# Splitting the first tile's window sums over VectorE and Pool, later softmax, one Exp, and new planner costs in a three-layer kernel

## The chip, the cores and the metric

The kernel runs on one core of one Trainium2 chip. The metric is the device time in microseconds of one execution; lower is better. Engines are named as in the profile: PE (TensorE, matrix products), DVE (VectorE), ACT (ScalarE), POOL (GpSimd, "Pool" in the text) and SP (SyncE, which issues all transfers here).

## What is computed

Three layers in a row on x of shape 2 x 4160 x 192, all float32:

```
w = softmax(weight_gen over its 7 taps)                 # [2, 4160, 8 heads, 7]
a[s] = sum over k of w[s, head, k] * x[s - 6 + k]       # a window of 7 rows, per head
prev = a shifted by one row
xk = mu_k * a + (1 - mu_k) * prev ;  xr = mu_r * a + (1 - mu_r) * prev
y = sigmoid(xr @ w_r) * (relu(xk @ w_k)**2 @ w_v)       # 192 -> 1024 -> 192
h = relu(y @ w_in) ;  c = 3-tap convolution of h along the rows, per channel
out = (h * sigmoid(c)) @ w_out                          # 192 -> 1024 -> 192
```

## The kernel before

**Tiles.** The 4160 rows are cut into ten tiles: 256, 248, seven of 472 and one of 352 rows, each for both batches. A tile holds 2, 2, 4, ..., 4, 3 "slots" per batch, one row of x per partition in each. For one slot and batch, `token` computes the window sum in four elementwise instructions: a product of 128 x 1344 elements (rows times softmax weights) into the scratch tile `prod`, and three sums of 576, 384 and 192 elements, the last into `tok`. `attention` loads the rows of one tile and batch in one transfer and issues its tokens; all of them run on Pool.

**From tokens to matrix products.** `mixing(i, u, ...)` transposes `tok` on PE for one of three column groups (u = 0: batch 0; u = 2: what is left of both batches; u = 1: batch 1), mixes each row with the one before it, and splits the results into a high and a low part (`hi` on ACT, `lo` on DVE or Pool), so that a float32 product can be made of several fp32r products. For u = 2 the parts are also moved between partitions by transfers into `xB`. `moe1` is one of eight 128-channel chunks of the second layer (PE into `pa`, ACT and DVE into `s`, PE into `am` and `ar`), `moe2` the same for the third layer (`pc`, `h`, `g`, `bm`, `br`).

**Weights.** The weights arrive as 64-bit numbers in `stage` and are converted on the chip: for each of 16 pieces, `narrow` is one ACT copy and five DVE instructions, and `split` adds an ACT copy and a DVE subtraction per part. `wkA`, `wkB`, `wv`, `wrA`, `wrB` serve `moe1`, `wiA`, `wiB`, `wo` serve `moe2`.

**Softmax.** It is done in four parts: tile 0, tile 1, tile 2, and tiles 3 to 9. Each part has the steps maximum (DVE reduce), subtract, Exp (ACT), sum (DVE reduce), a small add and a reciprocal (DVE), and multiply. Subtract and multiply run on DVE for tile 0 and on Pool otherwise. For tiles 3 to 9 the steps are issued in seven groups, one per tile, each with an Exp of its own; the scratch of these groups lies in `stage`, which the weight conversion uses first. ACT has Exp and Sigmoid in different tables, so an Exp between two chunks of `moe2` brings two table loads.

**Order.** Nothing is issued directly. Each step is put in a list with a due time (`at(t, fn, hold)`, where one unit is one chunk of `moe1`); negative times are the prologue. `Program.schedule` then plans the whole program with estimated costs: at each moment it takes the engine that can start first, and on it the ready instruction with the lowest due time. `hold` is an earliest planned time in microseconds. The plan decides only the order of instructions on each engine; on the chip every engine runs its list in order and waits for data. The plan treats Pool instructions and those DVE instructions that read two SBUF operands (or copy SBUF to SBUF) as excluding each other (`shares`, `port`).

The lines that set the prologue are these:

```
softmax(0, 0, slots[0], DVE, (-95, -94.9, ...), am_r.tiles[0])
attention(0, 0, -99.9, -90, 0.1, POOL)
attention(0, 1, -99.6, -83.7, 0.1, POOL)
prepare((-99.75, -99.7, -99.4), [(-82, chunk_rem(w_k, wkB, True)), (-81, chunk_in(w_k, wkA, 0)), (-0.5, chunk_out(w_v, wv, 0)), ...
```

Of the kernel before, what the change touches and what calls it, by code (L numbers as in the profile page):

```python
# [24 lines left out]
WIN = KS * DM  # L25
NF = DFF // 128
LAG = 10


def f(ap):  # L30
# [3 lines left out]
class Program:  # L34
# [37 lines left out]
    def cost(self, eng, method, out, ins, pointer):  # L72

        n = self.count(out)
        src = [self.space(x) for x in ins]
        if method == "dma_start":
            return 0.6, 0.0
        if eng == "PE":
            busy = max(n * 0.00045 + 0.002, 0.109)
            return busy, busy + 0.24  # L80
        if eng == "ACT":
            near = bool(src) and src[0] == "PSUM"
            p = 0.1 if pointer else 0.0
            return (0.06 if near else 0.09) + p + n / 1200, (0.2 if near else 0.24) + p + n / 1200
        if eng == "DVE":
            if method == "tensor_reduce":
                n = self.count(ins[0])
            if method == "reciprocal":
                return 0.07 + n / 160, 0.2 + n / 160
            if method in ("tensor_scalar", "tensor_copy", "memset") and "PSUM" not in src:  # L90
                return 0.07 + n / 1920, 0.2 + n / 1920
            stt = method == "scalar_tensor_tensor"
            return (0.13 if stt else 0.07) + n / 960, (0.26 if stt else 0.2) + n / 960
        if eng == "POOL":
            busy = 0.1 + (n / 455 if method == "tensor_tensor" else n / 270)
            return busy, busy + 0.12
        return 0.6, 0.6

    def schedule(self):
        n = len(self.ops)  # L100
        succ, left, ready, dur, late, moved = [[] for _ in range(n)], [0] * n, [0.0] * n, [0.0] * n, [0.0] * n, [0.0] * n
        shares = [False] * n
        log = {}
        for i, (eng, method, a, k, _, hold) in enumerate(self.ops):
            ready[i] = hold
            aps = [x for x in [*a, *k.values()] if hasattr(x, "tensor") and hasattr(x, "ap")]
            out = k["out"] if "out" in k else aps[0]
            ins = [x for x in aps if x is not out]
            dur[i], late[i] = self.cost(eng, method, out, ins, any(x is not None and x in ("scale",) and hasattr(k[x], "tensor") for x in k))
            if method == "dma_start":  # L110
                moved[i] = self.count(out) * out.ap[0][1] * 4 / 240e3 if self.space(out) != "DRAM" else self.count(ins[0]) * ins[0].ap[0][1] * 4 / 240e3

            src = [self.space(x) for x in ins if self.count(x) > 1]
            shares[i] = eng == "POOL" or eng == "DVE" and (
                src == ["SBUF", "SBUF"] or method in ("tensor_scalar", "tensor_copy") and self.space(out) == "SBUF" and src == ["SBUF"])
            before = set()
            for x, write in [(x, False) for x in ins] + [(out, True)]:
                name, p0, p1, f0, f1 = self.region(x)
                seen = log.setdefault(name, [])
                keep = []  # L120
                for e in seen:
                    j, w, q0, q1, g0, g1 = e
                    if (w or write) and p0 < q1 and q0 < p1 and f0 < g1 and g0 < f1:
                        before.add(j)
                        if write and p0 <= q0 and q1 <= p1 and f0 <= g0 and g1 <= f1 and j != i:
                            continue
                    keep.append(e)
                keep.append((i, write, p0, p1, f0, f1))
                log[name] = keep
            before.discard(i)  # L130
            left[i] = len(before)
            for j in before:
                succ[j].append(i)
        free = dict.fromkeys(self.real, 0.0)
        port, table = 0.0, None
        wires = dict.fromkeys(self.real, 0.0)
        open_ = {e: [] for e in self.real}
        for i in range(n):
            if not left[i]:
                open_[self.ops[i][0]].append(i)  # L140
        start = [0.0] * n
        for _ in range(n):
            t, eng = min((max(free[e], min(ready[i] for i in w)), e) for e, w in open_.items() if w)
            i = min((i for i in open_[eng] if ready[i] <= t), key=lambda i: (self.ops[i][4], i))
            open_[eng].remove(i)
            if shares[i]:
                t = max(t, port)
                port = t + dur[i]
            turn = 0.0
            if eng == "ACT" and self.ops[i][1] == "activation" and self.ops[i][2][2] in (ACTF.Exp, ACTF.Sigmoid):  # L150
                turn = 0.0 if self.ops[i][2][2] == table else 1.3
                table = self.ops[i][2][2]
            start[i] = t
            free[eng] = t = t + turn
            free[eng] += dur[i]
            end = t + late[i]
            if self.ops[i][1] == "dma_start":
                wires[eng] = max(wires[eng], t + dur[i] + 0.6) + moved[i]
                end = wires[eng] + 0.8
            for j in succ[i]:  # L160
                ready[j] = max(ready[j], t + dur[i] if eng == "PE" == self.ops[j][0] else end)
                left[j] -= 1
                if not left[j]:
                    open_[self.ops[j][0]].append(j)
        for i in sorted(range(n), key=lambda i: (start[i], i)):
            eng, method, a, k = self.ops[i][:4]
            getattr(self.real[eng], method)(*a, **k)  # L167
# [14 lines left out]
def conv_moe_kernel(ctx: ExitStack, tc: tile.TileContext, xp, wg_first, wg_rest, mus, w_k, w_v, w_r, w_in, conv_w, w_out, out):  # L182
# [11 lines left out]
    def ring(name, n, shape, dtype=F32):  # L194
        return Ring([new(f"{name}{j}", shape, dtype) for j in range(n)])
# [28 lines left out]
    rows_r = ring("rows", 2, [128, max(SLOTS) + PAD, DM])  # L224
    prod = new("prod", [128, WIN])
    tok_r = ring("tok", 2, [128, max(SLOTS), NB * DM])
    att_r = ring("att", 2, [128, NMAX])
    mk_r = ring("mk", 2, [128, NMAX])
    rm_r = [ring(f"rm{k}", 1, [128, NMAX], F32R) for k in range(2)]
# [14 lines left out]
    sm = []  # L244
# [14 lines left out]
    def at(t, fn, hold=0.0):  # L259
        plan.append((t, len(plan), fn, hold))  # L260
# [107 lines left out]
        w = sm[j][0]  # L368
        at(t, lambda: SP.dma_start(out=w.rearrange("p s k h -> p (s k h)"), in_=wg), hold)

    def softmax(j, a, b, eng, times, bank):

        w, m, z = (x[:, a:b] for x in sm[j])
        n = b - a
        if bank is not None:
            z = bank[:, :n * NH].rearrange("p (s h) -> p s h", s=n)

        def fold(dst, op):
            DVE.tensor_reduce(out=dst, in_=w.rearrange("p s k h -> p s h k"), op=op, axis=AX.X)

        def each(v, op):
            eng.tensor_tensor(w, w, v.unsqueeze(2).to_broadcast([128, n, KS, NH]), op=op)

        def s3():
            ACT.activation(w, w, ACTF.Exp)

        def s5():
            DVE.tensor_scalar(z, z, 1e-9, None, op0=ALU.add)
            DVE.reciprocal(m, z)

        for t, fn in zip(times, (lambda: fold(m, ALU.max), lambda: each(m, ALU.subtract), s3,
                                 lambda: fold(z, ALU.add), s5, lambda: each(m, ALU.mult))):
            at(t, fn)

# [4 lines left out]
    def attention(i, b, t_load, t, dt_, eng, hold=(0.0, 0.0)):  # L401
# [7 lines left out]
        def token(l):  # L409
            if i not in tok_t:  # L410
                tok_t[i] = tok_r()
            p = prod
            y = p.rearrange("p (k d) -> p k d", k=KS)
            w = sw[:, sum(slots[:i]) + b * L + l].unsqueeze(2).to_broadcast([128, KS, DM // NH, NH])
            eng.tensor_tensor(p.rearrange("p (k g h) -> p k g h", k=KS, h=NH),
# [299 lines left out]
                           pattern=[[-1, 128]], channel_multiplier=1)  # L715

    at(-101, identity)
    at(-100.5, consts)
    softmax_load(0, wg_first, -100)
    softmax(0, 0, slots[0], DVE, (-95, -94.9, -94.8, -94.7, -94.6, -94.5), am_r.tiles[0])  # L720
    attention(0, 0, -99.9, -90, 0.1, POOL)
    attention(0, 1, -99.6, -83.7, 0.1, POOL)
    softmax_load(1, wg_rest[:, :slots[1] * KH], -99.5)
    softmax(1, 0, slots[1], POOL, (-82.6, -82.5, -82.4, -82.35, -82.3, -82.25), ar_r.tiles[0])
    prepare((-99.75, -99.7, -99.4), [(-82, chunk_rem(w_k, wkB, True)), (-81, chunk_in(w_k, wkA, 0)),
                                     (-0.5, chunk_out(w_v, wv, 0)), (0.4, chunk_out(w_v, wv, 1)), (1.0, chunk_in(w_k, wkA, 1)),
                                     (1.4, chunk_out(w_v, wv, 2)), (2.4, chunk_out(w_v, wv, 3)), (3.4, chunk_r()),
# [1 line left out]
                                     (6.4, chunk_conv()), (7.0, chunk_in(w_in, wiA, 1)), (8.0, chunk_out(w_out, wo, 1)),  # L729
                                     (9.0, chunk_out(w_out, wo, 2)), (10.0, chunk_out(w_out, wo, 3))])  # L730
    softmax_load(2, wg_rest[:, slots[1] * KH:(slots[1] + slots[2]) * KH], -99.3)
    softmax(2, 0, slots[2], POOL, (0.9, 0.91, 0.92, 0.93, 0.94, 0.95), None)
    softmax_load(3, wg_rest[:, (slots[1] + slots[2]) * KH:], 10.2, 40.0)
    for j in range(NTILE - 3):
        a, b = (sum(slots[3:3 + k]) for k in (j, j + 1))
        softmax(3, a, b, POOL, (16.5 + 0.3 * j, 16.6 + 0.3 * j, 19.5 + 0.1 * j, 20.5 + 0.5 * j, 20.6 + 0.5 * j, 24.9 + 16 * j), None)
    mixing(0, 0, -88, 0.1)
    mixing(0, 2, -75, 0.1)
    mixing(0, 1, -70, 0.1)
# [87 lines left out]
```

## Time and profile before

| | |
|---|---|
| three timed runs | 791.1, 791.6 and 793.21 us, median 791.6 us |
| the profiled execution: its own time | 793.36 us |
| the profiled execution: span, first to last instruction | 791.6 us |
| busy in the span: PE, ACT, DVE, POOL | 697.2, 666.5, 631.4, 506.2 us |
| mean granted TensorE clock | 0.973 |

The profiled execution's own time is 1.76 us above its span, and 1.76 us above the median of the timed runs. Almost all instructions carry line 167, that of the planner's issuing loop, so groups are told apart by tiles. Times in the views count from the start of the span.

### The profile page before, as it was taken

What the parts mean: (1) busy time and instruction counts of PE and PEld (TensorE: products, weight loads), DVE (VectorE), ACT (ScalarE), POOL (GpSimd) and SP (SyncE); (2) the same over time, 40 slices, a digit from 0 to 9 for tenths busy, and PEclk for the clock granted to TensorE, in tenths of its full rate; (3) what the DMA queues carried; (4) which work ended last, traced back from release to release, by engine and by line L of the source; (5) the groups of instructions that cost most, each with busy time, mean ns of one, the idle gap of its engine ahead of it and who ended that gap; (6) DMA issues with size and microseconds to landing.
All of it is one profiled execution on the core that took longest, in us unless ns stands there. A gap on an engine that the chain in (4) does not pass through costs nothing.

```text
span 791.6 us, 10781 instructions
## 1 busy us (share of the span) xinstructions
PE 697.2 (88%) x3505; PEld 607.3 (77%) x3505; DVE 631.4 (80%) x1137; ACT 666.5 (84%) x1441; POOL 506.2 (64%) x368
## 2 busy tenths in 40 slices
PE   0066776999999999999999999999999999999964
PEld 0054675898888888888888888888888888889843
DVE  5987977887878787878877887879787878788764
ACT  2467798998989899989898989989898989899854
POOL 5898888899999999999999789295401101000000
PEclk9997786999999999999999999999999999999998
DMA  7685010130130112112121211020002000100000
GB/s 202 194 277 174 13 51 11 58 103 10 61 99 19 51 69 59 59 51 91 28 69 51 68 46 58 7 68 1 20 12 56 20 1 21 35 19 1 20 14 14
DMA packets 19241, 45.09 MB, mean 57 GB/s; under 512 B 3057, under 2 KB 14705, under 8 KB 19057
## 3 DMA queue, kind: packets, MB, share of 16 engines
q1 hardware_dynamic: 19184, 44.41, 18.9%
q8 instruction: 27, 0.44, 0.2%
q14 instruction: 30, 0.24, 0.1%
HBM read 27.40 MB, written 6.39 MB: 43 GB/s over the span
## 4 chain that ended last, share of the span: by engine, by line
PE 68%; ACT 15%; DVE 13%; issue 2%; DMA 2%; SPq 0%; ACTq 0%; DVEq 0%
PE pa L167 21%; PE pc L167 16%; PE am L167 10%; PE bm L167 9%; PE ar L167 7%; PE br L167 5%; DVE pc L167 4%; ACT pa L167 2%; ACT pc L167 2%; DVE stage L167 2%; ACT h L167 2%; ACT g L167 2%; ACT L167 1%; DMA stage<-in_moe_w_k_dram 1%; DVE bm L167 1%
## 5 line engine op out<-in xcount | busy, mean ns | idle before, releaser
L167 DVE SCALAR_TENSOR_TENSOR pc<-h,cw,pc 128x472 f32<-128x472 f32 (+3 forms) x320 | 208.1, 650 | 39.5 <-ACT pc L167 36.7
L167 POOL TENSOR_TENSOR prod<-rows,sw 128x1344 f32<-128x1344 f32 x70 | 216.1, 3087 | 12.8 <-DMA rows<-in_x_dram 7.8
L167 ACT ACTIVATE pa<-pa 128x472 f32<-128x472 f32 (+3 forms) x320 | 160.8, 505 | 39.1 <-PE pa L167 35.2
L167 POOL TENSOR_TENSOR prod<-prod 128x576 f32<-128x576 f32 (+1 forms) x140 | 171.0, 1221 | 8.6
L167 PE MATMUL bm<-g,wo 128*128 128x472 f32 (+3 forms) x480 | 148.7, 360 | 21.3 <-ACT g L167 21.1
L167 PE MATMUL am<-s,wv 128*128 128x472 f32 (+3 forms) x480 | 147.0, 367 | 7.1 <-ACT s L167 5.8
L167 DVE TENSOR_TENSOR pc<-h,pc 128x472 f32<-128x472 f32 (+3 forms) x160 | 94.7, 592 | 59.2 <-ACT pc L167 57.9
L167 PE MATMUL pa<-xA,wkA 128*128 128x472 f32 (+3 forms) x480 | 125.9, 368 | 7.5 <-DVE s L167 3.4
L167 PE MATMUL pc<-x,wiA 128*128 128x474 f32 (+3 forms) x480 | 121.6, 361 | 3.5 <-DVE g L167 3.5
L167 POOL TENSOR_TENSOR xA<-mk,xA 128x472 fp32r<-128x472 f32 (+2 forms) x36 | 40.4, 1128 | 123.1 <-ACT xA L167 96.6
L167 PE MATMUL ar<-s,wv 128*128 128x472 f32 (+3 forms) x320 | 112.6, 364 | 4.9 <-DVE x L167 3.3
L167 PEld LDWEIGHTS bm<-g,wo 128*128 128x128 f32 x480 | 88.3, 191 | 35.4 <-ACT g L167 26.0
L167 PE MATMUL br<-g,wo 128*128 128x472 f32 (+3 forms) x320 | 112.4, 355 | 1.4 <-DVE ob L167 1.4
L167 DVE TENSOR_TENSOR s<-pa,s 128x472 fp32r<-128x472 f32 (+3 forms) x160 | 93.7, 586 | 16.8 <-ACT s L167 15.8
L167 DVE TENSOR_TENSOR g<-pc,g 128x472 fp32r<-128x472 f32 (+3 forms) x160 | 93.8, 586 | 15.5 <-ACT g L167 14.0
L167 PEld LDWEIGHTS am<-s,wv 128*128 128x128 f32 x480 | 89.1, 197 | 21.4 <-ACT s L167 11.0
L167 PEld LDWEIGHTS pa<-xA,wkA 128*128 128x128 f32 x480 | 87.6, 199 | 19.9 <-DVE s L167 6.4
L167 ACT ACTIVATE pc<-h,cw 128x472 f32<-128x472 f32 (+3 forms) x160 | 99.7, 623 | 1.8
L167 PEld LDWEIGHTS pc<-x,wiA 128*128 128x128 f32 x480 | 85.7, 193 | 15.9 <-DVE g L167 5.8
L167 ACT ACTIVATE h<-pc 128x474 f32<-128x474 f32 (+3 forms) x160 | 84.4, 527 | 11.4 <-PE pc L167 8.3
L167 ACT ACTIVATE pc<-pc 128x472 f32<-128x472 f32 (+3 forms) x160 | 80.9, 506 | 14.0 <-DVE pc L167 13.0
L167 PE MATMUL pa<-xB,wkB 128*128 128x472 f32 (+3 forms) x320 | 89.8, 362 | 1.5 <-DMA xB<-mk 1.5
(105 smaller groups left out, 1066.4 us busy)
## 6 DMA issues: line engine op xcount, KB each, us to landing
rows<-in_x_dram SPq DMA_DIRECT2D x14, 960.0 KB, 4.5
xB<-rm SPq DMA_DIRECT2D x28, 118.0 KB, 2.3
xB<-mk SPq DMA_DIRECT2D x28, 118.0 KB, 2.3
out_dram<-om SPq DMA_DIRECT2D x14, 236.0 KB, 2.0
rows<-in_x_dram SPq DMA_DIRECT2D x4, 768.0 KB, 7.1
rows<-in_x_dram SPq DMA_DIRECT2D x2, 864.0 KB, 4.5
out_dram<-ob SPq DMA_DIRECT2D x14, 118.0 KB, 2.2
stage<-in_moe_w_v_dram SPq DMA_DIRECT2D x4, 384.0 KB, 3.9
```

The source lines that it names most:

```text
L167: getattr(self.real[eng], method)(*a, **k)
```

## The change

Five things change. (1) Batch 0 of tile 0 has its two tokens on DVE, with `prod0`, the second `tok` buffer (first needed for tile 1), as scratch; batch 1 stays on Pool. (2) Its rows are loaded before the first softmax weights and before `mu`. (3) Pool's tokens of batch 1, and the softmax of tiles 1, 2 and 3 to 9, get a planned earliest time of 16.5 us. (4) Tiles 3 to 9 get one Exp over all seven groups, due at 19.5, after all their subtractions. (5) The planner counts a Pool instruction 0.05 us longer but its result as late by 0.02 us less, passes from one Pool instruction to a dependent one without that lateness, and for due times under -80 may choose an instruction that becomes ready within 0.2 us.

```diff
+AHEAD = 0.2
...
-            busy = 0.1 + (n / 455 if method == "tensor_tensor" else n / 270)
-            return busy, busy + 0.12
+            busy = 0.15 + (n / 455 if method == "tensor_tensor" else n / 270)
+            return busy, busy + 0.1
...
-            i = min((i for i in open_[eng] if ready[i] <= t), key=lambda i: (self.ops[i][4], i))
+            i = min((i for i in open_[eng] if ready[i] <= t + (AHEAD if self.ops[i][4] < -80 else 0.0)), key=lambda i: (self.ops[i][4], i))
+            t = max(t, ready[i])
...
-                ready[j] = max(ready[j], t + dur[i] if eng == "PE" == self.ops[j][0] else end)
+                ready[j] = max(ready[j], t + dur[i] if eng in ("PE", "POOL") and eng == self.ops[j][0] else end)
...
+    prod0 = tok_r.tiles[1].rearrange("p a b -> p (a b)")[:, :WIN]
...
-    def softmax(j, a, b, eng, times, bank):
+    def softmax(j, a, b, eng, times, bank, hold=0.0):
...
-            at(t, fn)
+            if t is not None:
+                at(t, fn, hold)
...
-            p = prod
+            p = prod0 if eng is DVE else prod
...
-    at(-100.5, consts)
+    at(-99.8, consts)
...
-    attention(0, 0, -99.9, -90, 0.1, POOL)
-    attention(0, 1, -99.6, -83.7, 0.1, POOL)
+    attention(0, 0, -100.1, -90, 0.1, DVE)
+    attention(0, 1, -99.6, -83.7, 0.1, POOL, (0.0, 16.5))
...
-    softmax(1, 0, slots[1], POOL, (-82.6, -82.5, -82.4, -82.35, -82.3, -82.25), ar_r.tiles[0])
+    softmax(1, 0, slots[1], POOL, (-82.6, -82.5, -82.4, -82.35, -82.3, -82.25), ar_r.tiles[0], 16.5)
...
-    softmax(2, 0, slots[2], POOL, (0.9, 0.91, 0.92, 0.93, 0.94, 0.95), None)
+    softmax(2, 0, slots[2], POOL, (0.9, 0.91, 0.92, 0.93, 0.94, 0.95), None, 16.5)
...
-        softmax(3, a, b, POOL, (16.5 + 0.3 * j, 16.6 + 0.3 * j, 19.5 + 0.1 * j, 20.5 + 0.5 * j, 20.6 + 0.5 * j, 24.9 + 16 * j), None)
+        softmax(3, a, b, POOL, (16.5 + 0.3 * j, 16.6 + 0.3 * j, None, 20.5 + 0.5 * j, 20.6 + 0.5 * j, 24.9 + 16 * j), None)
+    at(19.5, lambda: ACT.activation(sm[3][0], sm[3][0], ACTF.Exp))
```

## Rows read from the trace of the kernel before

**Rows 1.** Windows: length, busy time (instructions) of each engine, clock, DMA share, GB/s

```profile
12.30:40.00 27.70, 2.24 (x6) 0.94 (x6) 27.14 (x54) 9.81 (x23) 24.97 (x22) 1.00 0.68 198
40.00:60.00 20.00, 12.66 (x54) 11.34 (x53) 17.75 (x39) 12.16 (x35) 19.13 (x15) 1.00 0.88 277
60.00:70.00 10.00, 7.47 (x47) 5.87 (x46) 5.73 (x18) 7.60 (x23) 6.41 (x7) 0.98 0.81 261
70.00:100.00 30.00, 19.52 (x103) 17.37 (x104) 28.40 (x61) 21.50 (x57) 26.80 (x23) 0.67 0.11 31
100.00:135.00 35.00, 24.10 (x139) 21.99 (x138) 26.99 (x60) 33.34 (x73) 30.50 (x23) 0.79 0.10 35
...
135.00:165.00 30.00, 27.88 (x215) 26.80 (x216) 24.23 (x59) 26.68 (x81) 27.74 (x20) 0.95 0.17 52
165.00:700.00 535.00, 531.39 (x2569) 460.62 (x2569) 433.98 (x726) 486.17 (x1002) 365.29 (x252) 1.00 0.15 45
```

**Rows 2.** Timeline of the prologue: start, duration, engine, instruction [idle before, releaser]

```profile
1.17 0.42 SPq L167 DMA_DIRECT2D sw<-in_first_dram  x1
...
1.63 0.43 SPq L167 DMA_DIRECT2D rows<-in_x_dram  x1
...
3.98 0.55 SPq L167 DMA_DIRECT2D rows<-in_x_dram  x1
4.57 0.48 SPq L167 DMA_DIRECT2D sw<-in_rest_dram  x1
...
7.89 0.39 DVE L167 TENSOR_TENSOR sw<-sw,smz 128x224 f32<-128x224 f32 x1
9.14 3.01 POOL L167 TENSOR_TENSOR prod<-rows,sw 128x1344 f32<-128x1344 f32 x1 [7.76 <-DMA rows<-in_x_dram]
...
12.30 0.70 DVE L167 TENSOR_SCALAR bm<-bm 128x512 uint32<-128x512 uint32 x1 [4.02 <-ACT bm L167]
...
15.45 3.03 POOL L167 TENSOR_TENSOR prod<-rows,sw 128x1344 f32<-128x1344 f32 x1
...
38.75 0.59 POOL L167 TENSOR_TENSOR tok<-prod 128x192 f32<-128x192 f32 x1
...
47.28 1.19 PE L167 MATMUL pa<-xB,wkB 128*128 128x256 f32 x4 [1.47 <-DMA xB<-mk]
```

**Rows 3.** DMA issues in short stretches of the prologue: KB, us to landing

```profile
sw<-in_first_dram SPq DMA_DIRECT2D x1, 112.0 KB, 3.7
...
rows<-in_x_dram SPq DMA_DIRECT2D x1, 768.0 KB, 7.3
...
rows<-in_x_dram SPq DMA_DIRECT2D x1, 768.0 KB, 10.6
...
sw<-in_rest_dram SPq DMA_DIRECT2D x1, 112.0 KB, 10.3
```

**Rows 4.** Groups of DVE instructions by form, 0 to 135: busy us, mean ns

```profile
L167 DVE TENSOR_TENSOR x<-bm,x 128x512 fp32r<-128x512 f32 x2 | 1.4, 686 | 0.1
```

**Rows 5.** Timeline of DVE and Pool around 120 us

```profile
114.83 0.19 DVE L167 TENSOR_SCALAR stage<-stage 128x64 f32<-128x64 f32 x1
...
118.67 3.06 POOL L167 TENSOR_TENSOR prod<-rows,sw 128x1344 f32<-128x1344 f32 x1
...
120.17 1.61 DVE L167 TENSOR_SCALAR stage<-stage 128x64 f32<-128x64 f32 x1
```

**Rows 6.** Groups of ACT instructions by form, 92 to 135 and 0 to 160

```profile
L167 ACT ACT_TABLE_LOAD x12 | 15.4, 1283 | 0.2
...
L167 ACT ACTIVATE sw<-sw 128x448 f32<-128x448 f32 x6 | 3.5, 578 | 0.1
...
L167 ACT ACTIVATE sw<-sw 128x224 f32<-128x224 f32 x2 | 0.8, 392 | 0.0
```

**Rows 7.** Waits between 100 and 135: total us, times, longest

```profile
DVE stage L167 <- ACT sw L167: 5.5, 5, 1.7
```

**Rows 8.** Window of 135 to 140, columns as in the first group

```profile
135.00:140.00 5.00, 5.00 (x32) 5.00 (x33) 2.94 (x8) 3.05 (x11) 4.92 (x4) 0.71 0.00 0
```

## The prediction

> **What bounds the kernel now.** I read the busy time in stretches first, then the timeline of the prologue, then the waits of the stretch in which ACT is full. From 165 us on PE is busy 531.4 of 535 us [rows 1]: the rest of the run is a fixed amount of PE work, and the time can only come from when that state begins. Ahead of it the bound changes three times. Up to 47 us PE waits for Pool's four tokens. Between 12.3 and 100 us it is DVE: 27.1 of 27.7, 17.8 of 20, 5.7 of 10 and 28.4 of 30 us, mostly weight conversion. Between 100 and 135 us ACT is busy 33.3 of 35 us while PE has 24.1. The reader is to see in [rows 1] that DVE, not Pool, is full in the stretch behind the one that the change speeds up. So I sum along DVE: between 12.3 and 135 us it works 27.14 + 17.75 + 5.73 + 28.40 + 26.99 = 106.0 us and idles 122.7 - 106.0 = 16.7 us, of which 35 - 26.99 = 8.0 behind 100 us and 8.7 ahead of it.
>
> **Tokens: what Pool loses.** Pool's tokens of tile 0 follow each other at 15.45 - 9.14 = 6.3 us, and the last ends at 38.75 + 0.59 = 39.3 us, with two small softmax parts of other tiles between them [rows 2]. After the change Pool has two tokens. Its first instruction, and everything queued behind it on Pool, waits for the rows of batch 1. They land at 3.98 + 10.6 = 14.6 us [rows 2, 3], and the bytes ahead of them stay the same. The planned earliest time of 16.5 orders instructions only; it holds nothing on the chip. So Pool ends at 14.6 + 2 x 6.3 = 27.2 us, 12.1 us sooner. From Pool's end to the first run of PE that needs everything (mixing and `xB`) it was 47.28 - 39.34 = 7.9 us [rows 2]; this gives 35.1 us for it. The softmax of tiles 1 and 2 then stands behind these tokens. Pool's lead covers it; without that cover Pool would wait for one chain of about the length of tile 0's softmax, 3.4 us (below), ahead of tile 1's tokens.
>
> **Tokens: what DVE takes on.** A DVE product of 224 elements from two SBUF operands takes 0.39 us [rows 2], a subtraction of 512 elements 0.686 us [rows 4]: 1.02 ns an element. For 1344, 576, 384 and 192 elements that is 1.53, 0.75, 0.56 and 0.36 us, 3.2 us a token, 6.4 us for two. The second row reads one operand from PSUM, so two SBUF operands of this size are an extrapolation.
>
> Their start needs rows and softmax. With the rows issued first they land some 0.9 us sooner than 1.63 + 7.3 = 8.9, at about 8.0 us. The weights landed at 1.17 + 3.7 = 4.87 us, and tile 0's softmax ended at 7.89 + 0.39 = 8.28, 3.4 us later [rows 2, 3]. If the transfer of the weights is not held by the rows ahead of it, the tokens start at about 8.5 us. If it is, as the 112 KB that were issued behind batch 1's rows landed at 4.57 + 10.3 = 14.9, 0.3 us after those rows [rows 2, 3], they start at 8.0 + 0.3 + 3.4 = 11.7 us. I take the middle, 10.1 us, and so the end at 16.5 us. Moving `mu` behind the weights costs nothing: 2 KB, first needed by the mixing, which comes behind the tokens.
>
> In front of the change DVE begins the conversion at 12.30 us, after 4.0 us of idling for the weights [rows 2]. Now that instruction, and behind it the whole conversion with ACT's copies and SP's `wkB` transfers, waits until 16.5 us: **+4.2 us** on DVE's line, with bounds of 8.5 + 6.4 - 12.3 = +2.6 and, if every Pool instruction of a token comes between those of DVE, 11.7 + 6.4 + 6.3 - 12.3 = +12.1.
>
> This last is the question of the port. A DVE instruction from SBUF to SBUF with one operand took 0.19 us beside an idle Pool and 1.61 us beside a product on Pool: it ended at 121.78, Pool's at 121.73 [rows 5]. That one waited for Pool. No row of before shows an instruction with two SBUF operands beside a working Pool, so the price lies between nothing and Pool's 6.3 us for a token. I take nothing into the forecast, since the first token is over before 14.6 us and only some 2 us of the second (10.1 + 6.4 against 14.6) lie beside Pool; the upper end goes into a rival. The Trainium skill, "SBUF — State Buffer", section "Who interferes with whom", speaks against the change: a DVE instruction with two SBUF inputs contends with a Pool instruction that reads SBUF, and the loser blocks for the whole instruction. By that rule the upper end would be the one to expect wherever the two overlap. The row above shows such a block for one operand; none here shows it for two.
>
> **One Exp.** Between 92 and 135 us ACT loads tables 12 times, 15.4 us, and has seven Exps, six of 0.578 us and a shorter one [rows 6]. From 224 to 448 elements Exp grows by 0.186 us, 0.83 ns an element, so 3024 elements take 0.392 + 2800 x 0.83 = 2.7 us. Ten loads go (12.8 us), and the seven Exps of some 3.95 us become 2.7: 14.1 us less on ACT. "ScalarE: Activation LUTs", section "What ACT_TABLE_LOAD costs", of the Trainium skill counts 2.66 us for a switch, with a drain; by it ten would be 26.6 us. The rows here have 1.283 us, and the sum goes by them.
>
> It is not a gain of 14.1 us, since with ACT relieved DVE has 27.0 us of work in those 35. What can go is DVE's idle time. Five waits of DVE for Exp cost 5.5 us [rows 7], 1.1 us for each round of 2 x 1.283 + 0.578 = 3.14 us, 35%. The single Exp with its two loads holds ACT for 5.3 us; the chunks of `moe2` and PE's `bm` products queue behind it, and the same 35% gives 1.9 us. It must also wait for all seven subtractions on Pool; the sums behind it are first used for tile 3, behind tile 2's eight tokens, so that is covered.
>
> **DVE's idle time.** Where the conversion is dense DVE idles 1.6 of 30 us [rows 1], 5.3%. In the changed kernel PE starts earlier while the conversion is later, so DVE should always find its next operand: 106.0 / 0.947 - 106.0 = 5.9 us, plus 1.9 for the single Exp, 7.8 in place of 16.7: **-8.9 us**. The other bound is that only the Exp waits go: 5.5 - 1.9 = -3.6.
>
> **Clock.** From 135 to 140 us PE is full at a granted clock of 0.71 [rows 8], after a stretch in which it was idle a third of the time. If PE is fed without those gaps this piece takes 5.0 x 0.71: **-1.4 us**, between 0 and that.
>
> **The planner.** A longer Pool, and no gap between dependent Pool instructions, change the order of Pool against DVE. Pool is busy 365 of the 535 us behind 165 [rows 1], so this is hidden there by PE's work; ahead of it I cost it at nothing, and if that cover fails it is one Pool instruction, 3 us, in front of a mixing. `prod0` is free again long before tile 1's first token.
>
> **Sum.** +4.2 - 8.9 - 1.4 = -6.1 us. The profiled execution took 793.36 us, 1.76 us around its span of 791.6, and would take 787.3; the median of the timed runs, 791.6, lies 1.76 below it, so the forecast is **785.5 us**.
>
> **Rivals.**
> *PE's earlier start is kept* (0.15). The weights do not wait for the rows, DVE's tokens end at 8.5 + 6.4 = 14.9 us, and DVE has no idle time but the Exp: 14.9 + 106.0 + 1.9 = 122.8 in place of 135, and the clock: -13.6 us, 778 us. For it: PE's first full run comes 12 us sooner. Against it: 5% of idling remained even where DVE was fullest.
> *Absorbed* (0.22). DVE's waits between 40 and 70 us are latencies of PE and ACT and come back, and PE's clock stays: +4.2 - 3.6 = +0.6, 792.2 us. For it: 6.5 of the 8.7 us of DVE's idle time ahead of 100 us lie there [rows 1]. This is also the case in which the change of engine does nothing, since Pool's time was not the bound.
> *Slower: the port* (0.16). DVE's instructions with two SBUF operands wait as the one of [rows 5] did: each of the second token's four instructions for one of Pool's, with nothing else allowed in between in DVE's order. The conversion then begins at 24.4 us, +12.1; with -8.9 of idle time, and the clock no better because PE starves for weights, this is +3.2 us, 794.8 us. It decides (more than 0.3%) from a start of the conversion at 12.3 + 8.9 + 2.4 = 23.6 us.
>
> **Chances and range.** A difference of 0.3%, 2.4 us, is about what a measurement of this kernel can tell from none. The forecast has 0.47, its own range 783 to 789 us. Faster by over 0.3% is this and the first rival, 0.62; no change 0.22; slower 0.16. The range from 778 (the first rival) to 795 us (the port) leaves out what lies past either.
>
> **What the new profile would show.** DVE's products of 1344 elements at about 1.5 us, starting between 8.5 and 11.7; longer than 2 us, or DVE instructions that end with Pool's, show the port. Pool's last token of tile 0 at about 27; PE's first `pa<-xB` at about 35; DVE's first conversion at about 16.5. Two table loads behind 90 us and one Exp of 2.7 us. DVE idling under 8 us up to the point where PE turns full, and that point at about 129 in place of 135. The forecast is wrong if the conversion starts later than 21 us, if DVE's waits for `s` in 40 to 70 us remain, or if PE turns full no sooner although its first run does.

## The result

The changed kernel takes 801.64 us, median of four runs, against 791.35 us for the kernel before: a ratio of 1.0133, 95% interval [1.0101, 1.0166]. It is 10.3 us slower; 785.5 us were forecast, with a range of 778 to 795. Its profiled execution took 800.95 us with a span of 799.1 us, 7.6 us more than the 793.36 us of the kernel before in its own profile. (That one stood 2.0 us above the median of its four runs, this one 0.7 us below.)

The windows of the changed kernel, with the columns and stretches of [rows 1] and [rows 8]:

```profile
12.30:40.00 27.70, 3.13 (x9) 1.65 (x9) 27.14 (x40) 7.20 (x18) 15.04 (x15) 1.00 0.37 94
40.00:60.00 20.00, 11.53 (x62) 9.96 (x62) 16.32 (x38) 11.03 (x32) 18.81 (x13) 1.00 0.98 299
60.00:70.00 10.00, 6.35 (x35) 5.04 (x35) 8.92 (x18) 8.05 (x21) 9.61 (x6) 0.89 0.46 169
70.00:100.00 30.00, 18.77 (x101) 16.40 (x101) 27.38 (x67) 19.90 (x60) 27.61 (x24) 0.69 0.53 142
100.00:135.00 35.00, 25.51 (x165) 22.55 (x165) 30.88 (x65) 27.49 (x70) 32.54 (x26) 0.90 0.08 26
135.00:140.00 5.00, 3.38 (x17) 3.38 (x18) 4.77 (x10) 0.95 (x3) 4.69 (x5) 0.66 0.15 65
135.00:165.00 30.00, 23.75 (x167) 21.64 (x168) 27.07 (x63) 21.46 (x66) 21.91 (x16) 0.94 0.05 18
165.00:700.00 535.00, 528.20 (x2552) 456.34 (x2552) 430.25 (x719) 482.73 (x995) 366.61 (x254) 1.00 0.15 45
```

Two stretches are worse. From 135 to 165 us, where PE was nearly full before (27.88 of 30 us [rows 1]), it has 23.75. And from 165 to 700 us, where PE's work should have been a fixed amount, it idles 6.8 us in place of 3.6. ACT is relieved as planned (27.49 of 35 us, before 33.34 [rows 1]), but DVE is busy 30.88 of them, before 26.99.

The timeline of the prologue, DVE and Pool, answering to [rows 2]:

```profile
8.10 1.56 DVE L170 TENSOR_TENSOR tok<-rows,sw 128x1344 f32<-128x1344 f32 x1
9.69 4.54 DVE L170 TENSOR_TENSOR tok<-tok 128x576 f32<-128x576 f32 x3
11.01 3.02 POOL L170 TENSOR_TENSOR prod<-rows,sw 128x1344 f32<-128x1344 f32 x1 [9.59 <-DMA rows<-in_x_dram]
14.10 3.66 POOL L170 TENSOR_TENSOR prod<-prod 128x576 f32<-128x576 f32 x2
14.27 2.64 DVE L170 TENSOR_TENSOR tok<-rows,sw 128x1344 f32<-128x1344 f32 x1
16.95 5.38 DVE L170 TENSOR_TENSOR tok<-tok 128x576 f32<-128x576 f32 x3
17.85 0.98 POOL L170 TENSOR_TENSOR tok<-prod 128x192 f32<-128x192 f32 x1
...
22.72 0.68 DVE L170 TENSOR_SCALAR bm<-bm 128x512 uint32<-128x512 uint32 x1
...
24.75 0.59 POOL L170 TENSOR_TENSOR tok<-prod 128x192 f32<-128x192 f32 x1
...
33.22 1.13 POOL L170 TENSOR_TENSOR sw<-sw,smz 128x448 f32<-128x448 f32 x1 [7.19 <-DVE smz L170]
...
37.96 0.66 POOL L170 TENSOR_TENSOR sw<-sw,smz 128x224 f32<-128x224 f32 x1 [3.61 <-DVE smz L170]
...
40.04 3.04 POOL L170 TENSOR_TENSOR prod<-rows,sw 128x1344 f32<-128x1344 f32 x1 [1.35 <-DMA rows<-in_x_dram]
```

A row with x3 is three instructions that the view joins. The first product on DVE runs alone: 1.56 us. The three sums behind it, some 1.7 us of work, take 4.54: they end at 14.23, and Pool's product ends at 14.03. Behind that the engines take turns. DVE's tokens end at 22.3 us and the conversion begins at 22.72, 10.4 us later than before. Pool suffers too: its two larger sums take 3.66 us, its 192-element sum 0.98 (0.59 in [rows 2]). The groups of DVE's token instructions by form, 8 to 22.5 us (busy us, mean ns), show which one pays:

```profile
L170 DVE TENSOR_TENSOR tok<-tok 128x192 f32<-128x192 f32 x2 | 6.2, 3104 | 0.1
L170 DVE TENSOR_TENSOR tok<-rows,sw 128x1344 f32<-128x1344 f32 x2 | 4.2, 2101 | 0.1
L170 DVE TENSOR_TENSOR tok<-tok 128x576 f32<-128x576 f32 x2 | 2.2, 1095 | 0.1
L170 DVE TENSOR_TENSOR tok<-tok 128x384 f32<-128x384 f32 x2 | 1.4, 694 | 0.1
```

The smallest sum is the dearest, 3.1 us, the length of a Pool product: what it costs is not its own size but the instruction of Pool that it meets.

Pool's lead is lost at the next step. It ends batch 1's tokens at 25.3 us, then waits 7.19 and 3.61 us for softmax steps of the next tiles that stand on DVE behind the conversion. Tile 1's first product starts at 40.04 us, no sooner than in the kernel before:

```profile
39.42 3.02 POOL L167 TENSOR_TENSOR prod<-rows,sw 128x1344 f32<-128x1344 f32 x1
```

The single Exp and its two table loads, from ACT's timeline, are as forecast:

```profile
117.77 1.28 ACT L170 ACT_TABLE_LOAD   x1
119.07 2.72 ACT L170 ACTIVATE sw<-sw 128x3024 f32<-128x3024 f32 x1
122.07 1.28 ACT L170 ACT_TABLE_LOAD   x1
```

Last, the new wait in PE's full stretch: the waits of PE, 165 to 500 us (us in total, times, longest), and the timeline around the longest:

```profile
PE pa L170 <- DVE mk L170: 2.5, 3, 1.4
```

```profile
298.53 3.10 POOL L170 TENSOR_TENSOR prod<-rows,sw 128x1344 f32<-128x1344 f32 x1
...
301.59 1.20 POOL L170 TENSOR_TENSOR xA<-mk,xA 128x472 fp32r<-128x472 f32 x1
...
302.82 0.71 DVE L170 SCALAR_TENSOR_TENSOR mk<-att,onemu,pa 128x472 f32<-128x472 f32 x1 [1.71 <-POOL xA L170]
...
303.58 0.91 PE L170 MATMUL pa<-xA,wrA 128*128 128x472 f32 x3 [1.39 <-DVE mk L170]
```

Read from the bottom: PE waits for a mixing on DVE, that for a small subtraction on Pool, and that stands behind a whole token product. Before, this stretch has no wait of PE for `mk`.

### The profile page after: what moved, and what is told of

Its sections match the earlier page's. It is cut to its first block, busy times and chain, and to the rows that moved or that the text cites. A ratio compares the mean times of both kernels' runs of the same rounds, so it can differ in the third digit from the quotient of the medians.

```text
span 799.1 us, 10761 instructions
## 1 busy us (share of the span) xinstructions
PE 696.9 (87%) x3505; PEld 602.9 (75%) x3505; DVE 645.5 (81%) x1145; ACT 654.4 (82%) x1425; POOL 496.2 (62%) x360
## 4 chain that ended last, share of the span: by engine, by line
PE 59%; DVE 15%; ACT 11%; POOL 10%; issue 3%; DMA 1%; ACTq 0%; SPq 0%; POOLq 0%; DVEq 0%
PE pa L170 17%; PE pc L170 14%; PE am L170 9%; POOL prod L170 8%; PE bm L170 8%; PE ar L170 6%; PE br L170 5%; DVE pc L170 4%; DVE stage L170 3%; ACT pc L170 2%; ACT pa L170 2%; ACT h L170 2%; ACT g L170 1%; DVE tok L170 1%; DVE g L170 1%
## 5 line engine op out<-in xcount | busy, mean ns | idle before, releaser
L170 POOL TENSOR_TENSOR prod<-rows,sw 128x1344 f32<-128x1344 f32 x68 | 210.1, 3089 | 16.0 <-DMA rows<-in_x_dram 10.9
L170 POOL TENSOR_TENSOR prod<-prod 128x576 f32<-128x576 f32 (+1 forms) x136 | 167.4, 1231 | 8.7
L170 PE MATMUL am<-s,wv 128*128 128x472 f32 (+3 forms) x480 | 146.7, 366 | 16.2 <-ACT s L170 10.4
L170 PEld LDWEIGHTS am<-s,wv 128*128 128x128 f32 x480 | 87.4, 193 | 32.3 <-ACT s L170 16.9
L170 DVE TENSOR_TENSOR s<-pa,s 128x472 fp32r<-128x472 f32 (+3 forms) x160 | 93.9, 587 | 16.3 <-ACT s L170 15.5
L170 DVE TENSOR_TENSOR g<-pc,g 128x472 fp32r<-128x472 f32 (+3 forms) x160 | 94.0, 587 | 15.8 <-ACT g L170 14.6
L170 PE MATMUL pa<-xB,wkB 128*128 128x472 f32 (+3 forms) x320 | 88.1, 356 | 3.1 <-DMA xB<-mk 3.1
```

## The experiments

Ratios are to the kernel before, run on the same chip, with 95% intervals. "Conversion end" is the end of DVE's last instruction for `wo`; "PE idle" is 535 us less PE's busy time from 165 to 700 us. Both are from the profiled execution. "Chaining" is the planner's passing from one Pool instruction to a dependent one without lateness, "look-ahead" its choice of an instruction that becomes ready within 0.2 us, "Pool cost" the new cost terms, "the add" the small number added to the softmax sums. Times of different calls were taken on different chips, where the kernel before had medians from 790.3 to 791.5 us, so a difference between two calls is uncertain by about 1 us. The intervals of e3 and e5 overlap with that of the changed kernel. The profiled execution of e5 took 803.38 us, 3.6 us more than the median of its runs.

| kernel | us | ratio | conversion end | PE idle |
|---|---|---|---|---|
| before | 791.35 | 1 | 89.4 | 3.6 |
| changed | 801.64 | 1.0133 [1.0101, 1.0166] | 99.3 | 6.8 |
| e1 before + single Exp | 782.65 | 0.991 [0.9889, 0.9932] | 85.4 | 3.8 |
| e2 before + DVE tokens | 797.77 | 1.008 [1.0065, 1.0095] | 98.2 | 4.3 |
| e3 changed, shared scratch | 798.43 | 1.0109 [1.0085, 1.0134] | 95.0 | 6.0 |
| e4 changed, batch 0 on Pool | 793.66 | 1.0041 [1.0024, 1.0059] | 84.1 | 9.3 |
| e5 changed, no softmax hold | 799.78 | 1.0107 [1.009, 1.0124] | 98.6 | 6.7 |
| e6 changed, seven Exps | 801.83 | 1.0144 [1.0114, 1.0175] | 98.1 | 6.5 |
| e7 changed, old planner | 794.01 | 1.005 [1.0028, 1.0073] | 96.3 | 3.8 |
| e8 e1 + new load order | 783.73 | 0.99 [0.9879, 0.992] | 83.4 | 3.7 |
| e9 before + planner | 807.0 | 1.0199 [1.0183, 1.0214] | 89.8 | 8.9 |
| e10 before + chaining alone | 800.08 | 1.0109 [1.0089, 1.013] | 91.2 | 11.3 |
| e11 before + Pool cost alone | 785.42 | 0.9924 [0.9904, 0.9944] | 84.9 | 3.4 |
| e12 e1 without the add | 780.1 | 0.9852 [0.9833, 0.9871] | 86.9 | 3.9 |
| e13 changed, no chaining | 802.02 | 1.0141 [1.0121, 1.0161] | 101.3 | 4.4 |
| e14 e13 + batch 0 on Pool | 786.37 | 0.9941 [0.992, 0.9962] | 86.4 | 4.7 |
| e15 e12 + Pool cost | 778.35 | 0.9835 [0.9814, 0.9855] | 84.9 | 3.7 |
| e16 e14 without the add | 782.42 | 0.9895 [0.9877, 0.9913] | 82.5 | 3.4 |
| e17 e13, no look-ahead | 792.94 | 1.0028 [1.0014, 1.0042] | 97.1 | 4.1 |
| e18 e13, old Pool cost | 794.82 | 1.0055 [1.0035, 1.0075] | 99.4 | 4.1 |

Two columns split without exception. The nine kernels with tokens on DVE end the conversion at 95 to 101 us, the others at 82 to 91. The seven with chaining have PE idle for 6.0 to 11.3 us behind 165, the others for 3.4 to 4.7. A wait of PE for `mk` behind 165 us splits them in the same way: the seven have one, 2.0 to 5.8 us in total, and none of the other thirteen has.

**The theory after the result**: the delay of the conversion by the port, and the planner, are prices of about equal size that hide a real gain of the single Exp. **The rival**: the order of DVE and Pool is upset by any of the changes, and no part can be told apart.

**The single Exp by itself (e1).**

```diff
-softmax(3, a, b, POOL, (..., 19.5 + 0.1 * j, ...), None)
+softmax(3, a, b, POOL, (..., None, ...), None)
+at(19.5, lambda: ACT.activation(sm[3][0], sm[3][0], ACTF.Exp))
```

> The kernel before with the single Exp alone. Port theory (the loss comes from DVE's and Pool's tokens blocking each other, which starts the conversion 10.4 us late): no loss here, DVE's idle time between 100 and 135 us falls from 8.0 to about 4, time 786 to 791 us. Rival (the single Exp waits for seven subtractions and pushes the sums behind 120 us): 796 us or more, with PE idle behind 130 us.

782.65 us, 7.7 us faster: somewhat better than expected. The window behind 100 us shows PE's work growing from 24.10 to 25.81 us, and DVE filling up from 26.99 to 31.08 [rows 1]:

```profile
100.00:135.00 35.00, 25.81 (x182) 24.09 (x182) 31.08 (x70) 27.50 (x72) 28.98 (x23) 0.90 0.02 6
```

**And inside the changed kernel (e6)**: the change with the seven Exps put back.

> The changed kernel with the seven Exps of before. If the single Exp is worth as much here as in the kernel before (7.7 us): 807 to 811 us. Rival (in the changed kernel DVE is behind anyway between 95 and 145 us, so ACT's relief is hidden): 800 to 804 us.

801.83 against 801.64 us: there the single Exp is worth nothing. With seven Exps DVE is busy 34.38 of the 35 us, so it is DVE's late work, not ACT, that sets the pace:

```profile
100.00:135.00 35.00, 22.98 (x135) 20.55 (x135) 34.38 (x63) 27.23 (x63) 31.90 (x25) 0.80 0.08 29
```

**The load order (e8)**: e1 with the rows loaded first, as in the change.

```diff
-at(-100.5, consts)
+at(-99.8, consts)
-attention(0, 0, -99.9, -90, 0.1, POOL)
+attention(0, 0, -100.1, -90, 0.1, POOL)
```

> The kernel before with the single Exp and with the changed order of the first transfers (rows before the first softmax weights, mu behind them). If the order of the transfers is harmless, as the softmax weights landed at 4.7 us in the changed kernel too: within 2.4 us of 782.7 us. Rival (it delays tile 0): 786 us or more.

783.73 us: the order does no harm.

**The tokens on DVE (e2, e3, e4).** e2 gives them alone to the kernel before (`attention(0, 0, -99.9, -90, 0.1, DVE)` with `prod0`).

> The kernel before with batch 0's two tokens on DVE and nothing else changed. Port theory: DVE's four instructions of the second token, and part of the first, wait for Pool's; the conversion's last piece ends 6 us or more later than in the kernel before, time 796 to 800 us. Rival (the tokens on DVE cost nothing by themselves, the loss is the planner's and the hold's): 788 to 792 us.

797.77 us: as expected, the price is 6.5 us. e3 takes away the overlap with Pool alone: DVE uses Pool's scratch, so that Pool can't start before it is done.

```diff
-p = prod0 if eng is DVE else prod
+p = prod
```

> The changed kernel with DVE's tokens in Pool's own scratch, so that Pool's first product has to wait until DVE's second token is done and the two never run side by side. Port theory: DVE's two tokens take 6.6 us in place of 14.2, the conversion starts at about 15.5 in place of 22.7, Pool's tokens start at about 15 and end at about 27.5; time 793 to 797 us. Rival (Pool's idle time behind its tokens, waiting for the softmax of tiles 1 and 2, is the loss): 800 us or more, since that waiting stays.

DVE's timeline in e3 shows what the same instructions take without Pool beside them:

```profile
8.49 1.56 DVE L170 TENSOR_TENSOR prod<-rows,sw 128x1344 f32<-128x1344 f32 x1
10.08 1.35 DVE L170 TENSOR_TENSOR prod<-prod 128x576 f32<-128x576 f32 x2
11.46 0.36 DVE L170 TENSOR_TENSOR tok<-prod 128x192 f32<-128x192 f32 x1
11.86 1.56 DVE L170 TENSOR_TENSOR prod<-rows,sw 128x1344 f32<-128x1344 f32 x1
...
15.57 0.69 DVE L170 TENSOR_SCALAR bm<-bm 128x512 uint32<-128x512 uint32 x1
```

1.56 + 1.35 + 0.36 = 3.3 us a token, and the conversion begins at 15.57 us, 7.15 us sooner than in the changed kernel, although Pool starts 4.3 us later than there. The port is thus shown as the cause of that delay of the start. But the conversion ends only 4.2 us sooner, and the time, 798.43 us, was above the expected 793 to 797 and below the rival's 800: less than half of the 7.15 us arrives. Without any overlap the tokens still hold DVE for 6.7 us, so most of what they cost in time is not shown to be the port. Pool's timeline in e3 speaks against the rival:

```profile
15.28 3.02 POOL L170 TENSOR_TENSOR prod<-rows,sw 128x1344 f32<-128x1344 f32 x1 [13.86 <-DVE tok L170]
...
33.36 3.04 POOL L170 TENSOR_TENSOR prod<-rows,sw 128x1344 f32<-128x1344 f32 x1 [1.80 <-DMA rows<-in_x_dram]
```

It waits only 1.2 us for the softmax of the next tiles, and its first product of tile 1 starts 6.7 us sooner than in the changed kernel and 6.1 sooner than in the kernel before. The time stays long even so. e4 puts batch 0 back on Pool (`attention(0, 0, -100.1, -90, 0.1, POOL)`), all else as changed.

> The changed kernel with batch 0's tokens back on Pool, all else as changed. Port theory: DVE's conversion starts at 9 to 12 us; time 787 to 793 us. Rivals: if the late softmax of tiles 1 and 2 or the single Exp is the loss, 798 us or more.

793.66 us, at the upper end of what was expected: the tokens on DVE cost 8.0 us here. The conversion starts at 8.51 us and ends at 84.1, 15 us sooner, yet PE idles 9.3 us behind 165. PE's waits there (columns as above) are again for `mk`:

```profile
PE pa L170 <- DVE mk L170: 5.3, 2, 2.8
```

**The planner (e7, e9, e10, e11).** e7 is the change with the planner's old costs, no chaining and no look-ahead; e9 the kernel before with all three new; e10 with the chaining alone; e11 with the cost alone.

```diff
-            busy = 0.1 + (n / 455 ...                       # e9, e11
-            return busy, busy + 0.12
+            busy = 0.15 + (n / 455 ...
+            return busy, busy + 0.1
...
-            ... if ready[i] <= t), ...                      # e9
+            ... if ready[i] <= t + (AHEAD if self.ops[i][4] < -80 else 0.0)), ...
...
-            ... if eng == "PE" == self.ops[j][0] else end)  # e9, e10
+            ... if eng in ("PE", "POOL") and eng == self.ops[j][0] else end)
```

> The changed kernel with the planner's costs, chaining and look-ahead as before. DVE then has conversion instructions between those of its tokens. Port theory: the tokens still block each other but the conversion goes on in between, so about half the delay is left, 794 to 799 us. Rival (the planner's new costs made the order worse everywhere): 791 us or less.

> The kernel before with the planner's new Pool cost, chaining and look-ahead alone. Planner theory (Pool's subtractions for the mixing come behind whole tokens, so that DVE waits for a free mk buffer and PE for DVE): PE waits of 1 us or more for DVE's mk between 200 and 500 us, 3 to 6 us in sum, time 793 to 797 us. Rival (the planner's costs matter only in the prologue): within 2.4 us of the kernel before, and no such waits.

> The kernel before, and of the planner's changes only the passing from one Pool instruction to a dependent one without lateness. If this is what packs Pool's tokens without a gap, so that Pool's mixing subtractions and DVE's small SBUF additions wait behind whole products: 798 to 808 us. Rival (the longer Pool costs do it): within 2.4 us of the kernel before.

> The kernel before, and of the planner's changes only the Pool cost (0.15 for 0.1, lateness 0.1 for 0.12). If the longer costs do the harm: 796 us or more. Rival (the chaining does it): within 2.4 us of the kernel before.

The planner, costed at nothing, takes 7.6 us in the changed kernel (794.01 without it, at the lower end of what was expected for e7) and 15.7 us alone, more than either theory had; e9's wait for `mk` between 200 and 500 us, 2.0 us, is shorter than expected. The chaining alone costs 8.6 us; e10's PE idles 11.3 us behind 165, 5.8 of them in one wait for `mk`. The cost terms alone gain 6.0 us, which neither theory expected; in that order the seven Exps fall together in part and bring 6 table loads where there were 12 [rows 6]. In e9, besides `mk`, PE waits 13.0 us for ACT's `g` between 100 and 165 us, and the small additions of the softmax stand on DVE until Pool's product ends:

```profile
114.02 3.02 POOL L170 TENSOR_TENSOR prod<-rows,sw 128x1344 f32<-128x1344 f32 x1
...
114.79 2.31 DVE L170 TENSOR_SCALAR stage<-stage 128x64 f32<-128x64 f32 x1
...
134.19 3.01 POOL L170 TENSOR_TENSOR prod<-rows,sw 128x1344 f32<-128x1344 f32 x1
...
134.53 2.72 DVE L170 TENSOR_SCALAR stage<-stage 128x48 f32<-128x48 f32 x1
```

The two end at 117.04 and 117.10, and at 137.20 and 137.25 us: the same block as in [rows 5]. Four of the five such additions between 112 and 138 us took 1.49 us or more.

**The add (e12).** It is left out of the softmax: 1e-9 on sums that are 1 or more.

```diff
-DVE.tensor_scalar(z, z, 1e-9, None, op0=ALU.add)
```

> The kernel before with the single Exp and without the addition of 1e-9 to the softmax sums, which are at least 1, so that float32 keeps the same value. In the run with the single Exp alone these seven small additions of tiles 3 to 9 took 3.7 + 1.5 us on DVE beside Pool. If DVE is the bound between 85 and 135 us: 777 to 781 us. Rival (PE is fed there by something else): 781.5 to 784 us, as with the single Exp alone.

780.1 us, as expected and 2.6 us below e1; PE has 28.89 us in the window of 100 to 135, e1 25.81.

**The hold (e5)**: the softmax of tiles 1 and 2 without its earliest time (`16.5` dropped from both calls). The change gives an earliest time to these and to batch 1's tokens of tile 0 alone; for tiles 3 to 9, 16.5 is the due time at which their steps begin, as before.

> The changed kernel without the earliest time of 16.5 for the softmax of tiles 1 and 2 and without another change. If Pool's idle time behind its two tokens (7.2, 3.6 and 1.4 us of waits) is what costs: 794 to 797 us, with Pool's first token of tile 1 some 8 us sooner. Rival (Pool has slack there, DVE's late conversion is the bound): 799 to 803 us.

799.78 us: at most 1.9 us back, as the rival had it. But the run does not take away Pool's idling: Pool still waits 4.10 and 3.61 us for DVE's softmax steps, and its first token of tile 1 starts at 38.37 us, 1.7 us sooner and not 8. That this idling is not the loss rests on e3.

**Which part of the planner, in the changed kernel (e13, e14, e17, e18).** e13 takes the chaining out of the change; e14 also puts batch 0 on Pool; e17 and e18 take the look-ahead or the cost out of e13.

> The changed kernel without the planner's chaining of dependent Pool instructions; the higher Pool cost and the look-ahead stay. Theory: the chaining is the part of the planner that costs (alone in the kernel before it cost 8.6 us, the cost terms alone gained 6.0), so this comes to about 793 us, like the changed kernel with the whole old planner (794.0 us, 1.005), or below. Rival: the planner's price in the changed kernel belongs to the cost terms or the look-ahead, or to any other order: 798 us or more.

> The changed kernel without the chaining and with batch 0 of the first tile back on Pool. Theory: the delay of the conversion and the chaining are the two prices, each 7 to 8 us; without both the single Exp's gain of 7.7 us shows: 781 to 787 us. Rival: the price belongs to any disturbance of the order of DVE and Pool, and one removal already takes back what there is: 791 us or more.

> The changed kernel without chaining and without the look-ahead of 0.2 us; the higher Pool cost stays. Theory: the look-ahead lets DVE take the steps of the first softmax and the tokens back to back, ahead of every instruction of the conversion (with the old planner the conversion began at 9.10 us, between them), so the look-ahead is what costs here: about 794 us, conversion from about 9 us. Rival: the cost terms are the price: about 802 us, as without the chaining alone.

> The changed kernel without chaining and with the old Pool cost; the look-ahead stays. Theory (the look-ahead is the price): about 802 us, conversion from about 22 us, behind the tokens. Rival (the cost terms are the price): about 794 us.

e13 refutes the theory that chaining is the planner's price there: 802.02 us. PE idles 2.4 us less behind 165, as without chaining everywhere, but the conversion ends 2 us later still and the gain is gone. e14 fits the theory, at the upper end: 786.37 us, so with the conversion early, removing the chaining is worth 7.3 us (e4 to e14), and with the chaining gone the tokens on DVE cost 15.7 us (e13 to e14). e17 and e18 don't choose between look-ahead and cost: without either one the time falls by 9.1 and 7.2 us. Only together are they dear. What the look-ahead does is plain in e17's timeline:

```profile
8.77 0.70 DVE L169 TENSOR_SCALAR bm<-bm 128x512 uint32<-128x512 uint32 x1 [1.45 <-ACT bm L169]
...
11.12 1.55 DVE L169 TENSOR_TENSOR tok<-rows,sw 128x1344 f32<-128x1344 f32 x1
12.58 0.68 DVE L169 SCALAR_TENSOR_TENSOR stage<-stage,pc 128x512 f32<-128x512 uint32 x1
13.18 2.98 DVE L169 TENSOR_TENSOR tok<-tok 128x576 f32<-128x576 f32 x1
16.08 0.69 DVE L169 TENSOR_TENSOR bm<-bm,stage 128x512 f32<-128x512 f32 x1
```

Without it conversion and tokens alternate from 8.77 us on, and one sum instead of several meets a Pool product (2.98 us). With it the tokens run as one block, and the conversion begins behind them (at 22.72 us in the changed kernel). The start of the conversion does not decide by itself: in e7 and e17 it begins at 9.10 and 8.77 us, sooner than in the kernel before, and still ends at 96.3 and 97.1, 6.9 and 7.7 us later. What the nine kernels with a late end have in common is the time that DVE spends on the tokens. But e18, whose conversion begins at 20.4 us behind the block, is as good as e7: it ends its conversion when the changed kernel does (99.4 and 99.3 us) and takes 6.8 us less. So this end is not by itself the cause either; why cost and look-ahead are dear only together stays open.

**The best version (e15, e16).** e15 is e12 with the new Pool cost; e16 is e14 without the add.

> The kernel before with the single Exp, without the small add in the softmax of all parts (an output change far below rounding, the sums being 1 or more), and with the new Pool cost terms. If the cost terms' gain of 6.0 us alone was a gain of its own it adds to 780.1: 774 to 777 us. If it came from the Exps that happened to be grouped in that order (six table loads instead of twelve), it adds nothing: 779 to 783 us.

> As the changed kernel without chaining and with batch 0 on Pool, and without the small add in the softmax. If the add costs 3.7 us wherever DVE is the bound, this is 2 to 4 us below that kernel; if what the add cost was a wait in one order, within 1.5 us of it.

e15, 778.35 us, is the fastest kernel here, about 13 us under the kernel before and 23 under the changed one; it lies between the two expectations, and from e12 (0.9852 against 0.9835) it can't be told apart. So the cost terms' 6.0 us are mostly no gain of their own beside the single Exp. e16 is 4.0 us below e14: the add costs that much in this order too.

## Why the prediction was wrong

**The sum, term by term.** From 12.3 to 135 us DVE works 110.6 us and idles 12.1, against 106.0 and 16.7. From 12.3 to 22.25 it is held by the tokens, 9.9 us, so by 135 us it has done 110.6 - 9.9 = 100.7 us of the other work: 5.3 us behind. With the 3.2 us of new idling of PE behind 165 that is 8.5 us, against 7.6 measured between the two profiles. PE's busy time says much the same: by 165 us it has worked 89.0 us in place of 93.9, 4.8 us less, and with the 3.2 that is 8.0 (not corrected for the granted clock, 0.89 before and 0.91 changed up to there).

| term | forecast | measured |
|---|---|---|
| conversion late on DVE's line | +4.2 | +9.9 (its start: +10.4) |
| DVE's idle time | -8.9 | -4.6 |
| clock from 135 to 140 us | -1.4 | 0: PE is busy 3.38 of 5 us, at 0.66 |
| planner | 0 | +3.2 behind 165; what it adds ahead of that is not told apart from the first two |

**The step that failed first: "I take nothing into the forecast" for the port.** It rested on Pool's rows landing at 14.6 us and DVE's tokens starting at 10.1. The tokens started at 8.10 us, below the lower bound of 8.5, since the softmax weights did not wait for the rows. But Pool started at 11.01 us, 3.6 us sooner than taken, so five of DVE's eight instructions lay beside Pool, and not only the last 2 us. And the bound stood in the text: a block for the whole of Pool's instruction, the upper end +12.1. The Trainium skill, "SBUF — State Buffer", section "Who interferes with whom", says that the loser of such a pair blocks for the whole instruction. The trace agrees, now for two operands: 3104 ns for a sum that takes 0.36 us alone. The cost of a token itself was right (3.3 us, forecast 3.2), and e3 shows the conversion at 15.57 us without the overlap, inside the forecast's bounds. What the port costs in time is open: e3 gives back 3.2 us of the 8.0 that the tokens on DVE cost (e4), and it also starts Pool later.

**The second: "DVE should always find its next operand".** Of 8.9 us only 4.6 came. DVE's idle time fell by 3.9 us between 100 and 135 us and by 3.2 between 60 and 70, a stretch that the prediction counted among those that DVE fills although it was busy 5.7 of 10 us there; it grew by 1.4 between 40 and 60 and by 1.0 between 70 and 100. Its waits for ACT's `s` between 40 and 70 us, before and changed, stayed as they were, and the wait for the single Exp behind 100 us took 3.1 us where 1.9 were forecast (us in total, times, longest):

```profile
DVE s L167 <- ACT s L167: 3.0, 3, 1.3
DVE s L170 <- ACT s L170: 2.9, 3, 2.0
DVE stage L170 <- ACT sw L170: 3.1, 1, 3.1
```

Nothing of the delay was made up on the way: the conversion starts 10.4 us late and ends 9.9 us late. The single Exp's own step was right in kind and low in size (alone 7.7 us), but inside the changed kernel worth nothing (e6), since DVE had become the bound there. Its gain and the delay were added as if they were independent; they share DVE's time behind 100 us.

**The third: "I cost it at nothing" for the planner.** The cover named, PE's fixed work behind 165 us, does not hold. The price given if it fails, one Pool product of 3 us ahead of a mixing, is what the trace shows (298.53, 3.10 us), but in that very stretch. Each of the seven kernels with chaining has PE wait for `mk` there, and no other has; why the plan then sets the product ahead of the subtraction is only argued: in its times the subtraction's operand is not ready yet.

**Pool's lead** was real at 25.3 us (forecast 27.2) and was lost at once. "Pool's lead covers it" counted the softmax chain alone at 3.4 us; its steps wait their turn on DVE behind the conversion, and Pool waited 10.8 us. PE's first `pa<-xB` came at 45.0 us, forecast 35.1, as the mixing's DVE instructions stand there too. In e3, e2 and e17 it came at 37.4 to 37.9 us, and they are slower than the kernel before all the same (ratios 1.0109, 1.008 and 1.0028): this first run does not set the time.

**The rivals.** "Slower: the port" named the mechanism, at 794.8 us; it decided from a start of the conversion at 23.6 us, and this came at 22.7. It fell short of the time because it kept the -8.9 and left out the planner. "PE's earlier start is kept" (778 us) and "Absorbed" (792.2 us) are refuted by the time, and by DVE's windows: it still idles 12.1 us, and of its idle time only 4.6 us went. All three signs of being wrong that the prediction named came: the conversion started later than 21 us, the waits for `s` stayed, and PE turned full no sooner.

**What stays open**: the effects don't add. The tokens on DVE cost 6.5, 8.0 or 15.7 us, the planner 7.6 or 15.7, chaining 0, 7.3 or 8.6, depending on what stands beside them; and the joint price of cost and look-ahead has no place in the trace that was shown to be its cause.

## What to carry to other kernels

Before work is split over VectorE and Pool, lay their SBUF instructions side by side in time: a small sum or addition on VectorE with its operands in SBUF was held until the Pool product that it met had ended. Work that moves to an engine which is full in the next stretch delays all of that stretch, and a gain on another engine is then no longer a gain. A planner's cost terms are part of a change: run them by themselves before they are counted as nothing.

## What the runs showed of the hardware

The block at the port goes both ways. Beside DVE's tokens Pool's pair of sums took 3.66 us, in e3 without them 2.47, and its 192-element sum 0.98 against 0.59. On DVE an addition of 48 elements took 2.72 us beside a Pool product of 3.01 us, and one of 64 took 0.19 us beside an idle Pool [rows 5].

Transfers at the start land at other times from kernel to kernel. The transfer of batch 1's rows, issued at 3.98 us in both kernels, took 10.6 us before [rows 3]; in the DMA view of the changed kernel (KB, us to landing) it took 6.9:

```profile
rows<-in_x_dram SPq DMA_DIRECT2D x1, 768.0 KB, 6.9
```

And in e1, whose load order is that of the kernel before, 8.5:

```profile
rows<-in_x_dram SPq DMA_DIRECT2D x1, 768.0 KB, 8.5
```

The same order thus gave landings 2 us apart, and one profile's landing was taken as fixed. The start of the conversion, which waits for weights, moves with them: it is 12.30 us in the kernel before and 9.42 to 11.27 us in e1, e9, e10, e11, e12 and e15, which have the same load order and the same tokens on Pool. Against these the changed kernel starts it 11.5 to 13.3 us late, not 10.4.
